# One core, a linear attention and a gated feed-forward layer in float32: blocks 3 to 8 worked in pairs of 1024 tokens, both weights in the seven-product form

## The chip, the core and the metric

The kernel runs on one core of a Trainium2 chip. A core has five engines, each with its own queue of instructions that it works through in order: TensorE (PE, matrix products, with a separate row PEld for loading the stationary operand), VectorE (DVE), ScalarE (ACT), GpSimd (POOL) and SyncE (SP), which here only starts DMA transfers. Engines wait for one another through semaphores. SBUF is the on-chip memory, PSUM the eight banks into which TensorE accumulates, DRAM the memory off the core. The metric is the device time of one execution in microseconds (us); lower is better.

## The reference

```python
kv = np.einsum('bhsd,bhse->bhde', k, v)              # (8, 8, 64, 64)
out = np.einsum('bhsd,bhde->bhse', q, kv)            # no softmax
rms = np.sqrt(np.mean(out * out, axis=-1, keepdims=True) + 1e-06)
x = heads_side_by_side(out / rms * g_norm)           # (8, 576, 512)

h = x.transpose(0, 2, 1) @ U @ V                     # mixing along the 576 tokens, rank 32
u = x + h.transpose(0, 2, 1)
y = u + np.maximum(u @ w_ch1, 0.0) @ w_ch2           # 512 -> 2048 -> 512
```

All is float32. There are 8 batches of 576 tokens, 8 heads of 64 columns; the last line is by far the largest part. The fp32 products are made of three fp32r products each: every operand is split into a high and a low half, and hi*hi + hi*lo + lo*hi is kept.

## The kernel before

**Preparation.** A batch is prepared in four pieces, one per pair of heads (`pair_steps`): `kv` (k^T v, L277), `out` (q times that, L300, then the squares, the sums and the scaling, L303 to L331), `turn` (x is transposed in 32x32 pieces on DVE, L356, and 16 DMAs set the pieces into `ut32`, L359), `xsplit`, `t` (x^T U, L370) and `mix` (times V, L440, and a DVE addition to the turned x, L443). The steps' places are numbers in tables (`STEPS`, `PARTS`, `FIRST_KV`, `OTHER_KV`): so many half-iterations or stages after the start of a block.

**Feed-forward.** The 8*576 = 4608 tokens are worked in 9 blocks of 512, counted from 0 here as `j`. The hidden width of 2048 is cut into 16 chunks `f` of 128. For blocks 0 and 1, a chunk takes 12 matmuls of 512 columns (`ffn1`, L454 to L456: four row groups, three products each), a relu on ACT with the low half on DVE (L463, L464), and 12 matmuls for w_ch2 (`ffn2`, L471). For blocks 2 to 8 the first weight is used in a **seven-product form** (`fast_group`): two chunks and two halves of 256 tokens make a 2x2 problem of blocks, and seven products `P1` to `P7` replace eight. Each product is six matmuls of 256 columns (L607); DVE and ACT put the sums together (L662, L666, L669, L670). Their weight combinations are made in block 1 (`weight_combos`: POOL adds the two halves of each weight, L561; DVE makes four sums, L568), written to DRAM (`wd`) and read again for each block (`wt`, L597). Their token combinations are made by `factor` on DVE and ACT (L543 to L548). The second weight is used plainly there: 12 matmuls of 512 columns per chunk (L625), taken from `queue` between the products; the last block splits the last row group into two halves of 256 columns.

**What sets the order.** From block 2 on TensorE's order is the order of the code. On the other engines, and on TensorE in blocks 0 and 1, a scheduler chooses it when the program is built. SP starts all DMAs in one order; a DMA that waits holds up those behind it.

Of the kernel before, what the change touches and what calls it, by code (L numbers as in the profile page):

```python
# [73 lines left out]
def build(ctx: ExitStack, tc: tile.TileContext, kv_in, kvt0_in, kvt_in, q_in, uv_in, g_in, w_in, out):  # L74
# [20 lines left out]
    uf = const.tile([P, NT, 2 * R], F32, name="uf")  # L95
# [160 lines left out]
    def bank():  # L256
# [3 lines left out]
        return ps_p.tile([P, 512], F32, name="pp")  # L260

# [84 lines left out]

    def turn_step(b, p):
# [6 lines left out]
        else:  # L354
            xt = sc.tile([P, 4, NT, 32], F32, name="xt")
            nc.vector.transpose(out=xt.rearrange("p k i j -> p i k j"), in_=x.rearrange("p i (k j) -> p i k j", j=32))  # L356
            for a in range(4):
                for k in range(4):
                    nc.sync.dma_start(out=ut32[p][32 * k:32 * k + 32, QO[a]:QO[a] + QL[a]],  # L359
                                      in_=xt[32 * a:32 * a + 32, k, 0:QL[a] // 32].rearrange("p i j -> p (i j)"))  # L360

    def t_step(b, p):
        tp = bank()
# [71 lines left out]
    def mix_part(b, p, part):  # L435

        m = S // 2 if b < FAST else BLK * (b + 1) - S * b
        lo, hi = ((0, m), (m, S))[part]
        mp = bank()[:, 0:hi - lo]
        nc.tensor.matmul(mp, lhsT=state[b, p]["t4"], rhs=v4[:, lo:hi], start=True, stop=True)  # L440
        own = ut32[p][:, lo:hi]
        to = x32(b)[:, p, BLK - m:] if b >= FAST and part == 0 else own
        nc.vector.tensor_tensor(out=to, in0=mp, in1=own, op=ALU.add)  # L443
# [34 lines left out]
    def finish_part(part, j):  # L478
        c, cols, acc = part
        o = st.tile([P, DM], F32, name="st")[:, 0:cols.stop - cols.start]  # L480
        if j < FAST:
            uh, ul = ut[j]
            nc.vector.tensor_tensor(out=o, in0=acc, in1=uh[c].bitcast(F32), op=ALU.add)
            nc.gpsimd.tensor_tensor(out=o, in0=o, in1=ul[c].bitcast(F32), op=ALU.add)
# [32 lines left out]
    def ring(i):  # L517
# [8 lines left out]
        if i < 6:  # L526
            return slot(f"w1_{i - 4}", 1)[0]
# [539 lines left out]
```

## Time and profile before

| | |
|---|---|
| median of 3 runs (lowest to highest) | 909.07 us (908.11 to 911.46) |
| the profiled execution: its time / its span | 908.89 us / 907.1 us |
| DMA moved, mean rate | 186.81 MB, 206 GB/s |
| granted TensorE clock | 1.000 |

The span runs from the first to the last instruction of the profiled execution; the time has 1.8 us more around it. The profile's page gives the busy time of every engine, the costliest groups of instructions (line, engine, operation, output and input by the program's names, shape, count, busy time, mean of one, and the idle time before them with what ended it), the chain of work that ended last, and the DMAs. Matmuls overlap in their records, so the cost of one in a row of many is the distance from start to start, not its duration.

### The profile page before, as it was taken

Reading aid. Unit: us, or ns where it says so; the run is one execution under the profiler, and the core shown is the slowest. Engines: PE = TensorE matmul, PEld = TensorE weight load, DVE = VectorE, ACT = ScalarE, POOL = GpSimd, SP = SyncE. Lnnn points to the kernel's source line nnn. Section 1 sums busy time; section 2 is a strip of 40 time slices with the busy share of each in tenths; the row PEclk is TensorE's granted clock in tenths of the full one; section 3 lists DMA queues with packets and bytes.
Section 4 is the critical chain, followed back from the end, with each engine's and each line's share of the span. In section 5 each row is a group of like instructions: output and inputs, shape, how many; then the busy total and the mean of one; then the engine's idle time right before and its main releaser. Section 6 shows DMA issues by size and latency. Waiting matters only on the chain.

```text
span 907.1 us, 15333 instructions
## 1 busy us (share of the span) xinstructions
PE 888.4 (98%) x5540; PEld 788.2 (87%) x5540; DVE 569.8 (63%) x1278; ACT 368.3 (41%) x818; POOL 38.0 (4%) x53
## 2 busy tenths in 40 slices
PE   8899999999999999999999999999999999999997
PEld 7678888887889998899999999999999999998997
DVE  5799987668475577566856586558755662253233
ACT  5677743333244353444533354335332432232221
POOL 2000023212010000000000000000000000000000
PEclk9999999999999999999999999999999999999999
DMA  9966355544756565666665557557744665546541
GB/s 345 417 263 195 101 182 158 182 147 155 268 184 243 223 245 166 229 239 216 221 220 224 183 189 257 179 213 259 262 168 174 215 221 186 163 163 213 180 142 47
DMA packets 76541, 186.81 MB, mean 206 GB/s; under 512 B 12721, under 2 KB 45233, under 8 KB 69297
## 3 DMA queue, kind: packets, MB, share of 16 engines
q1 hardware_dynamic: 76464, 185.82, 58.3%
q8 instruction: 44, 0.72, 0.3%
q14 instruction: 33, 0.26, 0.1%
HBM read 149.73 MB, written 24.12 MB: 192 GB/s over the span
## 4 chain that ended last, share of the span: by engine, by line
PE 82%; DMA 7%; DVE 4%; SPq 3%; ACT 2%; issue 1%; POOL 0%; DVEq 0%; ACTq 0%
PE y L625 31%; PE h L607 15%; PE pp L607 14%; PE y L471 6%; SPq L359 3%; PE h L454 2%; PE pp L277 2%; PE h L455 2%; PE pp L300 2%; PE h L456 2%; DMA out<-st 1%; DMA wt<-wd 1%; DMA wd<-dec 1%; DMA ut<-xt 1%; DMA kvq<-kv_in 1%
## 5 line engine op out<-in xcount | busy, mean ns | idle before, releaser
L607 PE MATMUL h<-uc,wt 128*128 128x256 f32 x1176 | 175.2, 285 | 0.3 <-DVE sums L666 0.3
L625 PE MATMUL y<-hh,ws 128*128 128x512 f32 (+1 forms) x528 | 175.1, 389 | 0.0
L607 PE MATMUL pp<-uc,wt 128*128 128x256 f32 x1176 | 173.1, 283 | 0.1
L607 PEld LDWEIGHTS h<-uc,wt 128*128 128x128 f32 x1176 | 161.2, 190 | 10.2 <-DVE sums L666 0.7
L607 PEld LDWEIGHTS pp<-uc,wt 128*128 128x128 f32 x1176 | 154.9, 191 | 0.5 <-DVE sums L666 0.3
L625 PEld LDWEIGHTS y<-hh,ws 128*128 128x128 f32 x528 | 97.5, 189 | 16.2
L625 PE MATMUL y<-dec,ws 128*128 128x512 f32 (+1 forms) x396 | 103.0, 389 | 0.0
L625 PE MATMUL y<-hl,ws 128*128 128x512 f32 (+1 forms) x264 | 102.8, 389 | 0.0
L666 DVE TENSOR_TENSOR sums<-h,dec 128x256 f32<-128x256 f32 x112 | 47.1, 421 | 64.1 <-PE h L607 63.3
L625 PEld LDWEIGHTS y<-dec,ws 128*128 128x128 f32 x396 | 70.3, 189 | 11.9
L669 ACT ACTIVATE hh<-sums 128x512 fp32r<-128x512 f32 x75 | 47.0, 629 | 80.3 <-DVE sums L666 78.7
L666 DVE TENSOR_TENSOR sums<-pp,dec 128x256 f32<-128x256 f32 x112 | 47.1, 421 | 46.0 <-PE pp L607 39.8
L471 PE MATMUL y<-hh,ws 128*128 128x512 f32 x216 | 71.6, 397 | 0.2 <-ACT hh L463 0.2
L662 ACT COPY dec<-h 128x256 f32<-128x256 f32 x84 | 31.2, 372 | 86.2 <-PE h L607 85.9
L670 DVE SCALAR_TENSOR_TENSOR hl<-sums,hh 128x512 fp32r<-128x512 f32 x75 | 51.9, 692 | 18.9 <-ACT hh L669 18.2
L625 PEld LDWEIGHTS y<-hl,ws 128*128 128x128 f32 x264 | 49.9, 189 | 7.6
L454 PE MATMUL h<-ut,ws 128*128 128x512 f32 x112 | 44.9, 401 | 3.3 <-DVE hl L464 3.3
L471 PEld LDWEIGHTS y<-hh,ws 128*128 128x128 f32 x216 | 39.0, 188 | 8.0 <-issue 0.5
L455 PE MATMUL h<-ut,ws 128*128 128x512 f32 x112 | 43.8, 391 | 0.0
L456 PE MATMUL h<-ut,ws 128*128 128x512 f32 x112 | 43.7, 391 | 0.0
L471 PE MATMUL y<-hl,ws 128*128 128x512 f32 x108 | 42.0, 389 | 0.0
L316 DVE TENSOR_REDUCE sums<-x 128x10 f32<-128x640 f32 x28 | 22.9, 817 | 26.9 <-ACT x L304 26.6
(216 smaller groups left out, 1338.0 us busy)
## 6 DMA issues: line engine op xcount, KB each, us to landing
wt<-wd SPq DMA_DIRECT2D x56, 1024.0 KB, 5.8
wt<-wd SPq DMA_DIRECT2D x56, 768.0 KB, 5.2
kv_sb<-kv_in SPq DMA_DIRECT2D x29, 512.0 KB, 5.1
raw<-w_in SPq DMA_DIRECT2D x14, 1023.6 KB, 15.0
out<-st SPq DMA_DIRECT2D x35, 256.0 KB, 5.1
q_sb<-q_in SPq DMA_DIRECT2D x29, 288.0 KB, 5.6
wd<-ws SPq DMA_DIRECT2D x42, 128.0 KB, 3.8
ut<-xt SPq DMA_DIRECT2D x224, 20.0 KB, 2.1
```

Of the source, the lines that this page charges most:

```text
L316: nc.vector.tensor_reduce(out=sums.rearrange("p (i h) -> p i h", h=2), in_=xv, axis=AX.X, op=ALU.add)
L359: nc.sync.dma_start(out=ut32[p][32 * k:32 * k + 32, QO[a]:QO[a] + QL[a]], in_=xt[32 * a:32 * a + 32, k, 0:QL[a] // 32].rearrange("p i j -> ...
L454: nc.tensor.matmul(h, lhsT=w1s[f][0][:, d, :], rhs=uh[d], start=(d == 0), stop=False)
L455: nc.tensor.matmul(h, lhsT=w1s[f][0][:, d, :], rhs=ul[d], start=False, stop=False)
L456: nc.tensor.matmul(h, lhsT=w1s[f][1][:, d, :], rhs=uh[d], start=False, stop=(d == ND - 1))
L471: nc.tensor.matmul(acc, lhsT=w2s[f][w][:, c, :], rhs=h[:, cols], start=(f == 0 and w == 0 and h is hh), stop=(f == NF - 1 and w == 1))
L607: nc.tensor.matmul(acc, lhsT=w[:, ws_, e * P:(e + 1) * P], rhs=u[:, us, e, :], start=fresh and e == 0 and n == 0, stop=e == 1 and n == 2, ...
L625: nc.tensor.matmul(acc, lhsT=w2s[f][w][:, c, :], rhs=h[:, cols], start=start, stop=stop)
L662: return lambda acc: nc.scalar.copy(out=to, in_=acc)
L666: nc.vector.tensor_tensor(out=to, in0=acc, in1=other, op=ALU.add)
L669: nc.scalar.activation(out=hh, in_=sums[:, 1 - i], func=AF.Relu)
L670: nc.vector.scalar_tensor_tensor(out=hl, in0=sums[:, 1 - i], scalar=0.0, in1=hh.bitcast(F32), op0=ALU.max, op1=ALU.subtract)
```

## The change

- **Three plain blocks instead of two.** Block 2 is now worked like block 1 (`NC = 3`).
- **Blocks 3 to 8 in three pairs.** Within a pair the two halves are blocks of 512 tokens, and both weights are in the seven-product form. `UNITS` lists a pair's work: twice (s = 0 and 1) 28 units of the first weight (`first_unit`, L629) for four groups of two chunks, and then 28 units of the second weight (`second_unit`, L678). A unit is six matmuls of 512 columns.
- **Between the two**, the four hidden blocks of a group are kept as float32 (`hk`), relu is made in place by ACT (L639), POOL makes their combinations (L641, L642, L662, L664), and `make_part`, three units ahead, splits each factor of the second weight into high (ACT) and low (DVE, L660). POOL also adds the products that were set aside (`plus`, L689) and makes the differences of `factor` (L545). The outputs build up in the place of the input (`x32`) and leave from there (L699).
- **Weights.** `weight_combos` now runs for both weights, 16 times instead of 8, from block 1 into block 2; its four sums are POOL's (L579). All seven factors of both weights come from DRAM, four units (1 MB) a transfer, with three buffers (`load_units`, L598).
- **The turned x** goes to DRAM in four DMAs (L373) and comes back in one (L375).
- **Preparation** has new tables: batch 3 and 4 in blocks 1 and 2 (`EARLY`, `STARTS2`), batches 5 and 6 during pair 0, batch 7 during pair 1 (`STARTS`, in units).

```diff
-STEPS = dict(kv=1, out=2, t=8, mix=8, gap=6)
+STEPS = dict(kv=1, out=2, t=5, mix=7, gap=5)
...
+NC = 3
+PAIRS = 3
+KEEP = 4
+FIRST_COMBO = 1
+STARTS = {5: (2, 9, 16, 23), 6: (32, 44, 56, 64), 7: (8, 18, 56, 66)}
+PARTS = dict(kv=0, out=4, turn=8, xsplit=8, t=13, mix0=17, mix1=18)
+EARLY = {(3, 0): (dict(kv=21, out=22, xsplit=22, turn=22), dict(t=0, mix=4)),
+         (3, 1): (dict(kv=26, out=28), dict(xsplit=1, turn=1, t=6, mix=10))}
+STARTS2 = {(3, 2): 1, (3, 3): 9, (4, 0): 17, (4, 1): 25, (4, 2): 33, (4, 3): 41}
...
+USE2 = "P2 P1 P6 P5 P7 P3 P4".split()
+UNITS = [u for s in range(NG // KEEP)
+         for u in [("1", name, KEEP * s + g + i) for g in range(0, KEEP, 2)
+                   for two in (("P1", "P6") if g == 0 else ("P6", "P1"), ("P5", "P7"), ("P3", "P4"), ("P2",))
+                    for i in range(2) for name in two]
+         + [("2", name, KEEP * s + g) for name in USE2 for g in range(KEEP)]]
...
             for a in range(4):
-                for k in range(4):
-                    nc.sync.dma_start(out=ut32[p][32 * k:32 * k + 32, QO[a]:QO[a] + QL[a]],
-                                      in_=xt[32 * a:32 * a + 32, k, 0:QL[a] // 32].rearrange("p i j -> p (i j)"))
+                nc.sync.dma_start(out=xd[:, QO[a]:QO[a] + QL[a]].rearrange("(k j) n -> j k n", k=4),
+                                  in_=xt[32 * a:32 * a + 32, :, 0:QL[a] // 32].rearrange("p k i j -> p k (i j)"))
+            nc.sync.dma_start(out=ut32[p], in_=xd)
...
+        def less(name, a, b):
+            t[name] = st.tile([P, BLK], F32, name="st")
+            nc.gpsimd.tensor_tensor(out=t[name], in0=a, in1=b, op=ALU.subtract)
+            return t[name]
...
-            nc.vector.tensor_tensor(out=o, in0=a, in1=b, op=op)
+            nc.gpsimd.tensor_tensor(out=o, in0=a, in1=b, op=op)
...
+    def first_unit(q, g, name, w):
...
+        for e in range(2):
+            u = place(2 * USE.index(name) + e)
+            for n, (ws_, us) in enumerate(((0, 0), (0, 1), (1, 0))):
+                nc.tensor.matmul(acc, lhsT=w[:, ws_, e * P:(e + 1) * P], rhs=u[:, us], start=fresh and e == 0 and n == 0,
+                                 stop=e == 1 and n == 2, skip_group_check=not fresh)
...
+        if name in copies:
+            nc.scalar.copy(out=copies[name], in_=acc)
+            return
...
+        nc.vector.tensor_tensor(out=to, in0=acc, in1=other, op=ALU.add)
+        nc.scalar.activation(out=to, in_=to, func=AF.Relu)
+        if name == "P2":
+            nc.gpsimd.tensor_tensor(out=h12, in0=h22, in1=h12, op=ALU.subtract)
+            nc.gpsimd.tensor_tensor(out=kept_t(g), in0=h12, in1=h11, op=ALU.add)
...
+    def make_part(q, n):
...
+        nc.scalar.copy(out=hh, in_=src)
+        nc.vector.tensor_tensor(out=hl, in0=src, in1=hh.bitcast(F32), op=ALU.subtract)
+        if name == "P2":
+            nc.gpsimd.tensor_tensor(out=h21, in0=h21, in1=kept_t(g), op=ALU.subtract)
+        elif name == "P1":
+            nc.gpsimd.tensor_tensor(out=h11, in0=h22, in1=kept_t(g), op=ALU.subtract)
...
+    def second_unit(q, n, w):
...
+        def plus(to, s):
+            nc.gpsimd.tensor_tensor(out=to, in0=to, in1=s, op=ALU.add)
...
-    for what in queue:
-        what()
+    for q in range(PAIRS):
+        for n, (which, name, g) in enumerate(UNITS):
+            k = (q * NU + n) // 4
+            if n % 4 == 0:
+                for ahead in range(3):
+                    load_units(k + ahead)
```

How the rows of a queue stand before and after, at three places. First TensorE in the middle of a block. Before, in block 2: products of the first weight (L607, 256 columns) alternate with matmuls of the second (L625, 512 columns).

```order
L607 MATMUL h<-uc,wt 128x256 x6
L607 MATMUL pp<-uc,wt 128x256 x6
L625 MATMUL y<-dec,w2s_451 128x512 x7
L607 MATMUL h<-uc,wt 128x256 x6
L607 MATMUL pp<-uc,wt 128x256 x6
```

After, in pair 0, where the first weight's units (L629) end and the second's (L678) begin, with one piece of preparation (L286, L289, L455, L312) between them:

```order
L629 MATMUL y<-uc,wt 128x512 x6
L286 MATMUL pp<-tails 128x256
L289 MATMUL pp<-kv_sb 128x128 x4
L629 MATMUL y<-uc,wt 128x512 x18
L455 MATMUL h<-v_92,t_4094 128x288
L629 MATMUL y<-uc,wt 128x512 x6
L455 MATMUL h<-v_92,t_4094 128x288
L312 MATMUL pp<-kvb_94,q_sb 128x128 x4
L314 MATMUL pp<-kvb_94,q_sb 128x128
L678 MATMUL y<-hh,wt 128x512
L678 MATMUL y<-hl,wt 128x512
L678 MATMUL y<-hh,wt 128x512 x2
```

All matmuls of the feed-forward now have 512 columns, and the weights of both kinds are the streamed `wt`.

Second POOL. Before, its queue ends in block 2 with the last additions of `weight_combos` and of block 1's output:

```order
L561 TENSOR_TENSOR dec<-ws_1143 128x512
L561 TENSOR_TENSOR dec<-ws_1183 128x512
L561 TENSOR_TENSOR dec<-ws_1232 128x512
L561 TENSOR_TENSOR dec<-ws_1280 128x512
L484 TENSOR_TENSOR st<-st,ut 128x512 x4
```

After, it goes on through all pairs; here in pair 0, from the last group of the first half into its second units (`hk` the kept hidden blocks, `t` their combination, `sp` the products set aside, `x_2631` and `x_2632` the outputs of pair 0, `x_3738` and `x_3739` the input of pair 1):

```order
L642 TENSOR_TENSOR t_3902<-hk 128x512
L662 TENSOR_TENSOR hk<-hk,t_3902 128x512
L664 TENSOR_TENSOR hk<-hk,t_3902 128x512 x4
L689 TENSOR_TENSOR x_2631<-x_2631,sp 128x512 x2
L689 TENSOR_TENSOR x_2632<-x_2632,sp 128x512 x2
L545 TENSOR_TENSOR st<-x_3738 128x512
L689 TENSOR_TENSOR x_2631<-x_2631,sp 128x512 x2
L689 TENSOR_TENSOR x_2632<-x_2632,sp 128x512 x2
L641 TENSOR_TENSOR hk<-hk 128x512 x2
```

POOL has work beside every unit, and one subtraction for pair 1 (L545) stands before the second half's own.

Third SP. Before, the 16 DMAs of a turned x (L359) stand together between two weight transfers (L597):

```order
L597 DMA wt<-wd_98 128x2048
L359 DMA ut_86<-xt 32x160 x8
L359 DMA ut_86<-xt 32x128 x8
L597 DMA wt<-wd_98 128x1536
L183 DMA kv_sb<-kv_in 128x1024
```

After, in pair 0, four DMAs to DRAM (L373), then the one back (L375), which waits for those four; a weight transfer (L598), which waits for TensorE to free its buffer, can stand between them:

```order
L598 DMA wt<-wd_114 128x2048
L373 DMA xd_98<-xt 32x4x160 x2
L373 DMA xd_98<-xt 32x4x128 x2
L598 DMA wt<-wd_115 128x2048
L375 DMA ut_86<-xd_98 128x576
L192 DMA kv_sb<-kv_in 128x1024
```

The trip of a piece has become two transfers, one behind the other, and 5 DMAs stand where 16 stood.

More of the change, by code (lines that the diff above doesn't have):

```diff
@@ L345, in xsplit_step @@
         s["hl"] = (xh, xl)
+    xds = [tc.dram_tile([P, S], F32, name=f"xd{i}") for i in range(2)]
     def turn_step(b, p):
@@ L579, in make_room @@
-    def make_room(i):
-        if i > 0:
-            to = [whole(2 * i, 0, s) for s in range(2)]
+            nc.gpsimd.tensor_tensor(out=o, in0=a, in1=b, op=op)
+        for half, names in enumerate((("P5", "P6"), ("P7", "P3"))):
+            both = (const.tile([P, 2, 2, HALF], F32R, name="sh", tag="top") if half == 0
+                    else dec.tile([P, 2, 2, HALF], F32R, name="dec"))
+            src = t[:, 2 * half:2 * half + 2]
+            nc.scalar.copy(out=both[:, :, 0], in_=src)
+            nc.vector.tensor_tensor(out=both[:, :, 1], in0=src, in1=both[:, :, 0].bitcast(F32), op=ALU.subtract)
+            for k, name in enumerate(names):
+                put(name, None, both[:, k])
@@ L617, in y_of @@
-    def y_of(j):
-        return once(("y", j), lambda: outputs(j))
-    def ffn2_parts(j, hs, first, last):
-        def part(i, f, w, h, start, stop):
-            def run():
-                c, cols, acc = y_of(j)[i]
-                nc.tensor.matmul(acc, lhsT=w2s[f][w][:, c, :], rhs=h[:, cols], start=start, stop=stop)
-                if stop:
-                    finish_part((c, cols, acc), j)
-            return run
-        n = ND + (j == NBLK - 1)
-        halves = [range(2), range(2, n)] if last and len(hs) > 1 else [range(n)]
-        return [part(i, f, w, h, first and f == hs[0][0] and m == 0, last and f == hs[-1][0] and m == 2)
-                for some in halves for f, hh, hl in hs for i in some for m, (w, h) in enumerate(((0, hh), (0, hl), (1, hh)))]
@@ new lines, in at_block @@
+    def at_block(n, what):
+        later.setdefault((None, n), []).append(what)
+    at_block(3, lambda: [nc.gpsimd.tensor_copy(out=x32(0)[p][:, 0:UPPER[2]], in_=side(p)) for p in range(NPAIR)])
+    for (b, p), (_, at) in EARLY.items():
+        for name in at:
+            if name != "mix":
+                at_block(at[name], pair_steps(b, p)[name])
+        at_block(at["mix"], lambda b=b, p=p: mix_step(b, p))
+    for (b, p), start in STARTS2.items():
+        for at, what in pair_steps(b, p).items():
+            at_block(start + PARTS[at], what)
@@ new lines, in build @@
+    at_block(30, lambda: [factor(0, "P1 P2", e) for e in range(2)])
+    at_block(STARTS2[4, 2] + PARTS["mix1"] + 1, lambda: factor(0, "P5 P6 P7 P3 P4", 0))
+    at_block(STARTS2[4, 3] + PARTS["mix1"] + 1, lambda: factor(0, "P5 P6 P7 P3 P4", 1))
+    for b, starts in STARTS.items():
+        for p, start in enumerate(starts):
+            for at, what in pair_steps(b, p).items():
+                at_stage((b - 5) // 2, start + PARTS[at], what)
+    for b, at in CARRY.items():
+        for p in range(NPAIR):
+            at_stage((b - 4) // 2, at, lambda b=b, p=p: carry(b, p))
@@ L947, in build @@
+    for q in range(PAIRS - 1):
+        made = [(names, e) for names in ("P1", "P5 P6 P4", "P7", "P3", "P2") for e in range(2)]
+        for i, (names, e) in enumerate(made):
+            at_stage(q, MAKE[0] + MAKE[1] * i, lambda q=q, names=names, e=e: factor(q + 1, names, e))
     last = {}
```

383 lines of the change are left out of this document (191 added, 192 removed).

## The prediction

> **What bounds the kernel now.** I read the page's busy times and its chain first, then the table of stretches.
>
> ```profile
> PE 888.4 (98%) x5540; PEld 788.2 (87%) x5540; DVE 569.8 (63%) x1278; ACT 368.3 (41%) x818; POOL 38.0 (4%) x53
> PE 82%; DMA 7%; DVE 4%; SPq 3%; ACT 2%; issue 1%; POOL 0%; DVEq 0%; ACTq 0%
> ...
> 100.00:190.00 90.00, 88.88 (x451) 73.19 (x449) 69.70 (x140) 39.17 (x73) 18.05 (x14) 1.00 0.50 159
> 190.00:275.00 85.00, 82.94 (x458) 70.77 (x457) 55.64 (x111) 30.50 (x70) 13.30 (x10) 1.00 0.59 200
> 541.00:630.00 89.00, 89.00 (x599) 81.15 (x599) 56.90 (x136) 36.78 (x89) 0.00 (x0) 1.00 0.63 226
> 718.00:807.00 89.00, 89.00 (x559) 80.44 (x559) 41.35 (x90) 27.48 (x62) 0.00 (x0) 1.00 0.57 185
> ```
>
> A row of the table is a stretch and its length, then the busy time of PE, PEld, DVE, ACT and POOL, the granted clock, the DMA share and GB/s. In the middle of the kernel (541 to 630 us) TensorE is busy all the time at full clock, DVE 64% of it, and POOL does nothing. So time goes where matmuls go, and the other engines count only where they make TensorE wait. The two stretches to 275 us, blocks 1 and 2 of the old kernel, hold the only POOL work of the feed-forward, and TensorE idles there a little.
>
> **What a matmul costs.** The timeline of TensorE and the chain give the distances from start to start.
>
> ```profile
> 226.47 2.73 PE y L471 x12
> 237.36 2.72 PE y L471 x12
> ```
>
> ```profile
> 560.18 0.88 PE L607 MATMUL h<-uc,wt 128*128 128x256 f32 x6
> 560.89 0.88 PE L607 MATMUL pp<-uc,wt 128*128 128x256 f32 x6
> 561.61 1.55 PE L625 MATMUL y<-dec,ws 128*128 128x512 f32 x6
> 563.00 0.28 PE L274 MATMUL pp<-tails 128*128 128x256 f32 x1
> 563.11 1.05 PE L277 MATMUL pp<-kv_sb 128*128 128x128 f32 x8
> 563.92 0.31 PE L440 MATMUL pp<-v,t 128*128 128x128 f32 x1
> ```
>
> Twelve matmuls of 512 columns take 2.72 us of the chain: **0.227 us** each. Six of 256 columns take 561.61 - 560.89 = 0.72 us, or 0.715 by the mean of both rows: **0.119 us** each, over half of the other. (With their neighbours in between, six of 512 took 1.39 us, 0.232 each; the new units change bank as often, so I leave this out on both sides.)
>
> **The change, part 1: TensorE's work.** By the code, blocks 2 to 8 now hold 7 x 336 = 2352 matmuls of 256 columns (8 groups, 7 products, 6 each) and 7 x 192 = 1344 of 512 columns, 48 of them cut in two. That is 2352 x 0.119 = 279.9 us, and 1344 x 0.2268 + 48 x 0.011 = 305.3 us: 585.2 us. The new kernel has a third plain block, 384 x 0.2268 = 87.1 us, and three pairs with 112 units of 6, 2016 x 0.2268 = 457.2 us: 544.3 us. The difference is **-40.9 us**. Preparation keeps its matmuls. The gain has two sources: the second weight saves an eighth in six blocks, and 256 columns are no longer paid at over half of 512; block 2 gives some of it back. Since TensorE has no idle time to lose in the middle, all of it comes off the end, unless a new wait takes its place.
>
> **Part 2: POOL, and what it does to DVE.** This is where the profile speaks against the change. POOL's groups and one place in block 1:
>
> ```profile
> L561 POOL TENSOR_TENSOR dec<-ws 128x512 f32<-128x512 f32 x14 | 18.5, 1339 | 70.8 <-DVE dec L572 70.8
> L484 POOL TENSOR_TENSOR st<-st,ut 128x512 f32<-128x512 f32 x8 | 10.3, 1306 | 34.5 <-DVE st L483 34.5
> L543 DVE TENSOR_TENSOR t<-x,t 128x256 f32<-128x256 f32 x36 | 15.0, 417 | 0.6
> L321 DVE TENSOR_TENSOR ta<-ta,r 128x10 f32<-128x10 f32 x28 | 4.7, 168 | 0.6
> ```
>
> ```profile
> 207.88 2.84 POOL L561 TENSOR_TENSOR dec<-ws 128x512 f32<-128x512 f32 x2 [14.21 <-DVE dec L572]
> ...
> 208.18 1.40 DVE L543 TENSOR_TENSOR t<-x 128x256 f32<-128x256 f32 x1
> ...
> 209.50 1.24 DVE L320 TENSOR_TENSOR ta<-r,half 128x10 f32<-128x10 f32 x1
> ...
> 210.86 0.68 DVE L464 SCALAR_TENSOR_TENSOR hl<-h,hh 128x512 fp32r<-128x512 f32 x1
> ...
> 211.60 0.50 PE L454 MATMUL h<-ut,ws 128*128 128x512 f32 x1 [1.40 <-DVE hl L464]
> ```
>
> While POOL adds (207.88 to 210.72), a DVE subtraction that is worth 0.417 us takes 1.40, and one of ten columns, worth 0.168, takes 1.24. Both read two operands from SBUF. The next, L464, reads one from PSUM and takes its ordinary 0.68, but it stood behind them, and TensorE waited 1.40 us for it. So each POOL operation can cost DVE about 1 us if DVE meets it with such an instruction. The Trainium skill, page "SBUF — State Buffer", section "Who interferes with whom", has it as a lock: DVE with two SBUF inputs and a GpSimd instruction that reads SBUF take turns, and the second fully blocks. The rows agree.
>
> The new kernel counts 204 POOL operations of 128x512 (32 in `weight_combos`, 24 in `factor`, 96 on the kept blocks, 48 in `plus`, 4 at block 0's output) where 24 stood, and 64 of 128x256. The wide ones cost 1.31 to 1.34 us. No row has the narrow ones: they cost something between nothing and the 1.34 us of the wide ones, and I take half of these, 0.7, since they do half of the same work. That is 268 + 45 = 313 us where 32 were.
>
> *Blocks 1 and 2.* Sixteen combinations take 16 x (2 x 1.34 + 4 x 0.7) = 88 us of POOL where 8 x 2.68 = 21 stood, and four outputs move to DVE. What POOL cost TensorE so far:
>
> ```profile
> PEld h L454 <- DVE hl L464: 5.9, 7, 1.8
> ```
>
> 5.9 us in seven waits is an upper bound, as some have other causes; nothing is the lower. PE's own row of L454 puts 3.3 us to it.
>
> ```profile
> L454 PE MATMUL h<-ut,ws 128*128 128x512 f32 x112 | 44.9, 401 | 3.3 <-DVE hl L464 3.3
> ```
>
> With 67 us more POOL work beside two blocks, by ratio, 3.3 x 67 / 32 = 7 and 5.9 x 67 / 32 = 12; I take **+8 us**, from 3 to 20.
>
> *Pairs.* A unit takes 6 x 0.227 = 1.36 us. Per second unit DVE makes one low half, from two SBUF operands; per first unit at most one addition out of PSUM, which POOL doesn't hold up. The nearest rows:
>
> ```profile
> L170 DVE TENSOR_TENSOR xl<-x,xh 128x512 fp32r<-128x512 f32 x24 | 16.3, 678 | 2.8 <-ACT xh L158 2.8
> L329 DVE TENSOR_TENSOR x<-pp,half 128x512 f32<-128x512 f32 x28 | 19.3, 689 | 1.1
> L670 DVE SCALAR_TENSOR_TENSOR hl<-sums,hh 128x512 fp32r<-128x512 f32 x75 | 51.9, 692 | 18.9 <-ACT hh L669 18.2
> L669 ACT ACTIVATE hh<-sums 128x512 fp32r<-128x512 f32 x75 | 47.0, 629 | 80.3 <-DVE sums L666 78.7
> ```
>
> ACT has one operation of 0.63 us per unit and is no bound. The fullest stage for DVE is pair 0, with eight pieces of preparation. A piece costs DVE, by the last two stretches above, (56.90 - 41.35) / (136 - 90) x 16 instructions = 5.4 us, and TensorE some 2.8 (0.9 for kv by the rows from 563.00 on, as much for out, half a microsecond for t, the rest mix). Pair 0 takes TensorE 112 x 1.36 + 8 x 2.8 = 175 us. DVE has 56 x 0.68 + 32 x 0.69 + 14 x 0.69 + 16 x 0.7 = 81 us, and 8 x 5.4 = 43: 124. POOL's 56 operations, met at a random point, add half of 1.31 each, 37 us: 161 of 175. It fits, with little to spare. Parts are made three units (4.1 us) ahead, so single waits are covered; a crowded stretch is not. Pairs 1 and 2, with four pieces and none, stay at 81 + 22 + 37 = 140 of 164 and at 71 + 31 = 102 of 152. I take **+6 us** for all three, from 0 to the rival's 52 below.
>
> **Part 3: the streams.** A transfer of four units brings 1 MB in 4 x 1.36 = 5.4 us, with two buffers ahead.
>
> ```profile
> wt<-wd SPq DMA_DIRECT2D x56, 1024.0 KB, 5.8
> ...
> q_sb<-q_in SPq DMA_DIRECT2D x29, 288.0 KB, 5.6
> ...
> ut<-xt SPq DMA_DIRECT2D x224, 20.0 KB, 2.1
> ```
>
> Before, 1.75 MB came per group of 42 x 0.119 + 24 x 0.227 = 10.4 us, 168 KB per us; now 188. A transfer lands 5.8 us after its issue and has 10.8 us. The x that goes through DRAM needs two landings, 2.1 and about 5.6 (the one back is as large as a q), 7.7 us, plus at most one weight transfer between them on SP, 5.4: 13.1. From turn to mix there are 9 units, 12.3 us, and some preparation in between, 1 to 3 us. It just fits, so nothing is charged.
>
> **Part 4: ends.** Into pair 0 the first unit has TensorE's spare bank, and ACT's first copy waits for block 2's last chunk (2.7 us) with two units between; at the end the last output leaves in pieces of 256 instead of 128 KB. I take **+2 us** together, from 0 to 6.
>
> **The sum.** 907.1 - 40.9 + 8 + 6 + 2 = 882.3 us of span, and 1.8 us around it (908.89 - 907.1): **884 us**. The profiled run lies 0.2 us under the median of 909.07, so nothing is corrected.
>
> **Rivals.**
> *Slower: POOL and DVE take turns in earnest.* In the second 28 units of the second half of pairs 0 and 1, DVE has 28 x 0.68 + 14 x 0.69 = 28.7 us with two SBUF operands and POOL 24 x 1.31 = 31.4 us (8 on the hidden blocks, 8 `plus`, 8 in `factor`): in turns 60 us, beside 38.1 us of TensorE. That is 22 us over, twice; the other second halves have 16 POOL operations and are over by 2 each, 8 in all: +52 in the place of my +6, **930 us**. It decides once the excess of a stretch passes the 4.1 us of lead and the work can't move into the first units, where DVE reads PSUM. For it: the 1.40 and 1.24 us above. Against it: POOL's order has some of `factor` standing earlier, and POOL's late results are needed only units later. It is what the lock in the Trainium skill's page "SBUF — State Buffer" comes to here, taken at its word.
> *The gain mostly eaten by the x trip.* DVE waits in order for the x that comes back.
>
> ```profile
> DVE ut L443 <- DMA ut<-xt: 12.8, 8, 2.7
> ...
> DVE x L443 <- DMA ut<-xt: 4.6, 4, 2.1
> ```
>
> Now that is 17.4 us in 12 waits, hidden behind DVE's slack. If 13 us and more become usual, the 20 pieces from batch 3 on wait 1 to 2 us each, with DVE near full in pair 0: +20, **904 us**.
> *Nothing waits.* If the lead covers all of POOL, only the ends stay, 884 - 8 - 6: **870 us**.
>
> **Chances and range.** Forecast (871 to 898) 0.62; nothing waits (below 871) 0.08; the trip (898 to 912) 0.16; taking turns (912 to 940) 0.14. The range of 868 to 910 leaves out about 0.18: the last, the top of the trip, and little below. A measurement of this kernel can tell 0.5% from no change, 904.5 to 913.6 us. Faster: 0.62 + 0.08 + half of the trip, 0.78; within it: the other half, 0.08; slower: taking turns, 0.14.
>
> **What will show it.** Right: 512-column matmuls at 0.227 us through the pairs, a pair of about 153 us without and 175 us with preparation, DVE at 75 to 90% in pair 0, POOL near 310 us busy. In blocks 1 and 2, waits of TensorE for L482 of about 8 us. Wrong: waits of L678 for L660 with POOL busy beside them (the slower rival), DVE waiting at L462 for the transfer back (the trip), or L629 and L678 waiting for `wt`, which I left out.

## The result and the profile after

The changed kernel takes **923.69 us** (median of 4 runs, 923.10 to 924.11) against 908.86 us before in the same session: a ratio of 1.0158 with a 95% interval of 1.0137 to 1.0179. It is 14.8 us slower; 884 us were forecast. The time lies beside the 930 us of the rival "POOL and DVE take turns in earnest", which had a chance of 0.14.

First the page of the changed kernel, its busy times and its chain, as the prediction showed them of before.

```profile
PE 864.7 (94%) x4196; PEld 704.4 (76%) x4196; DVE 671.2 (73%) x1099; ACT 463.1 (50%) x890; POOL 357.8 (39%) x301
PE 47%; DVE 17%; DMA 2%; issue 2%; ACT 1%; SPq 0%; POOL 0%; DVEq 0%; ACTq 0%
```

The span is 921.1 us, against 907.1. TensorE's work did become less, but it is now busy 94% instead of 98% of the span, and DVE's share of the chain went from 4% to 17%. DVE executes fewer instructions than before (1099 for 1278), yet is busy 101 us longer: its instructions got longer, not more. The groups show which; of each the busy time, then the mean in ns.

```profile
L660 DVE TENSOR_TENSOR hl<-hk,hh 128x512 fp32r<-128x512 f32 x72 | 72.9, 1027 | 12.9 <-ACT hh L659 12.0
L660 DVE TENSOR_TENSOR dec<-hk,dec 128x512 fp32r<-128x512 f32 x72 | 67.6, 946 | 9.0 <-ACT dec L659 8.9
L660 DVE TENSOR_TENSOR dec<-t,dec 128x512 fp32r<-128x512 f32 x12 | 19.1, 1618 | 2.8 <-ACT dec L659 2.8
L554 DVE SCALAR_TENSOR_TENSOR uc<-st,g_sb,uc 128x512 fp32r<-128x512 f32 x24 | 30.3, 1264 | 1.9 <-ACT uc L553 1.8
L638 DVE TENSOR_TENSOR hk<-y,sp 128x512 f32<-128x512 f32 x92 | 62.7, 688 | 68.6 <-PE y L629 56.2
L689 POOL TENSOR_TENSOR x<-x,sp 128x512 f32<-128x512 f32 x48 | 75.6, 1598 | 68.3 <-DVE x L695 55.2 <-ACT sp L704 11.1 <-DVE half L334 2.0
```

L638 has one operand in PSUM and takes the 0.69 us that I had for all of them. L660 and L554 read two operands from SBUF and take 0.95 to 1.62 us. POOL's own additions went up as well, L689 from the 1.31 of the prediction to 1.60.

Next the view of TensorE's waits (total, times, longest).

```profile
PE y L678 <- DVE hl L660: 15.2, 8, 3.8
PE h L475 <- DVE hl L482: 9.5, 6, 4.0
PE h L455 <- DVE x L462: 8.6, 6, 4.2
```

All three are waits for DVE. The first is the sign that the prediction named for the slower rival; the second, 9.5 us, is near the 8 us that it named for its own forecast. The timeline in pair 0 shows how the first comes about (start, duration, instruction):

```profile
531.66 1.76 DVE L554 SCALAR_TENSOR_TENSOR uc<-st,g_sb,uc 128x512 fp32r<-128x512 f32 x1
533.35 0.74 DVE L554 SCALAR_TENSOR_TENSOR uc<-x,g_sb,uc 128x512 fp32r<-128x512 f32 x1
534.01 1.74 DVE L660 TENSOR_TENSOR hl<-hk,hh 128x512 fp32r<-128x512 f32 x1
535.68 1.77 DVE L554 SCALAR_TENSOR_TENSOR uc<-st,g_sb,uc 128x512 fp32r<-128x512 f32 x1
537.37 1.75 DVE L660 TENSOR_TENSOR hl<-hk,hh 128x512 fp32r<-128x512 f32 x1
```

```profile
533.57 1.64 POOL L545 TENSOR_TENSOR st<-x,x 128x512 f32<-128x512 f32 x1 [0.69 <-DVE uc L554]
535.17 1.73 POOL L642 TENSOR_TENSOR t<-hk 128x512 f32<-128x512 f32 x1
536.86 1.72 POOL L662 TENSOR_TENSOR hk<-hk,t 128x512 f32<-128x512 f32 x1
```

```profile
535.81 0.50 PE L678 MATMUL y<-hl,wt 128*128 128x512 f32 x1 [3.81 <-DVE hl L660]
```

From 534 us on each DVE instruction ends about half a microsecond after the POOL one that started before it, and the next of each starts at once: one pair per 1.7 us, where DVE alone needs 0.69. A second unit of TensorE needs one L660 per 1.36 us; with one L554 in between, DVE delivers one in 3.4 us. Ahead of the L660 that ends at 535.75 two L554 stood, and TensorE stood still for 3.81 us.

In blocks 1 and 2 the same happens on a smaller scale:

```profile
197.10 1.17 DVE L332 TENSOR_TENSOR ta<-r,half 128x10 f32<-128x10 f32 x1
198.30 1.20 DVE L333 TENSOR_TENSOR ta<-ta,r 128x10 f32<-128x10 f32 x1
...
200.62 0.67 DVE L482 SCALAR_TENSOR_TENSOR hl<-h,hh 128x512 fp32r<-128x512 f32 x1
```

```profile
196.95 2.53 POOL L571 TENSOR_TENSOR dec<-ws 128x512 f32<-128x512 f32 x2 [1.46 <-DVE dec L585]
```

```profile
201.35 0.50 PE L475 MATMUL h<-ut,ws 128*128 128x512 f32 x1 [2.38 <-DVE hl L482]
```

Two DVE instructions of ten columns, worth 0.17 us each, take 1.17 and 1.20: they end when the two POOL additions end, at about 198.2 and 199.5. L482 stands behind them and three more of the same piece of preparation, and TensorE waits 2.38 us.

The balance over the whole span: I summed, over all neighbouring matmuls, the distance from start to start less the bare one (0.227 us for 512 columns, 0.119 for 256). Gaps over 0.3 us went from 16.2 to 59.5 us, time at half clock from 0 to 7.0, smaller delays from 20.3 to 25.7: 92.2 us above the bare matmuls instead of 36.5, so 55.7 more. The span grew by 14.0, so the bare matmuls saved 41.7, at the prediction's own prices for one matmul. The prediction had 40.9.

### The profile page after: what moved, and what is told of

The parts are those of the page before. It is cut to its first block, busy times and chain, and to the rows that moved or that the text cites. A ratio compares the mean times of both kernels' runs of the same rounds, so it can differ in the third digit from the quotient of the medians.

```text
span 921.1 us, 12302 instructions
## 1 busy us (share of the span) xinstructions
PE 864.7 (94%) x4196; PEld 704.4 (76%) x4196; DVE 671.2 (73%) x1099; ACT 463.1 (50%) x890; POOL 357.8 (39%) x301
## 4 chain that ended last, share of the span: by engine, by line
PE 47%; DVE 17%; DMA 2%; issue 2%; ACT 1%; SPq 0%; POOL 0%; DVEq 0%; ACTq 0%
PE y L629 18%; PE y L678 15%; PE y L489 4%; DVE dec L660 4%; DVE hl L660 4%; DVE uc L554 2%; PE pp L312 2%; DVE hk L638 1%; PE pp L289 1%; PE h L475 1%; PE h L476 1%; PE h L477 1%; DMA out<-x 1%; DVE x L693 1%; DVE xt L370 1%
## 5 line engine op out<-in xcount | busy, mean ns | idle before, releaser
L629 PE MATMUL y<-uc,wt 128*128 128x512 f32 x966 | 229.9, 393 | 1.0 <-ACT sp L635 1.0
L629 PEld LDWEIGHTS y<-uc,wt 128*128 128x128 f32 x966 | 178.7, 188 | 37.9 <-ACT sp L635 1.4
L678 PE MATMUL y<-dec,wt 128*128 128x512 f32 x504 | 128.8, 399 | 1.4 <-DVE dec L660 0.7
L678 PEld LDWEIGHTS y<-dec,wt 128*128 128x128 f32 x504 | 94.2, 191 | 27.9 <-DVE dec L660 9.0
L678 PE MATMUL y<-hh,wt 128*128 128x512 f32 x336 | 114.0, 397 | 0.0
L638 DVE TENSOR_TENSOR hk<-y,sp 128x512 f32<-128x512 f32 x92 | 62.7, 688 | 68.6 <-PE y L629 56.2
L641 POOL TENSOR_TENSOR hk<-hk 128x512 f32<-128x512 f32 x24 | 31.6, 1316 | 184.4 <-ACT hk L639 184.4
L689 POOL TENSOR_TENSOR x<-x,sp 128x512 f32<-128x512 f32 x48 | 75.6, 1598 | 68.3 <-DVE x L695 55.2
L639 ACT ACTIVATE hk<-hk 128x512 f32<-128x512 f32 x96 | 60.3, 630 | 52.9 <-DVE hk L638 51.6
L678 PE MATMUL y<-hl,wt 128*128 128x512 f32 x168 | 68.2, 406 | 15.6 <-DVE hl L660 15.2
L660 DVE TENSOR_TENSOR hl<-hk,hh 128x512 fp32r<-128x512 f32 x72 | 72.9, 1027 | 12.9 <-ACT hh L659 12.0
L660 DVE TENSOR_TENSOR dec<-hk,dec 128x512 fp32r<-128x512 f32 x72 | 67.6, 946 | 9.0 <-ACT dec L659 8.9
L678 PEld LDWEIGHTS y<-hh,wt 128*128 128x128 f32 x336 | 64.2, 191 | 12.8
L489 PEld LDWEIGHTS y<-hh,ws 128*128 128x128 f32 x336 | 62.0, 188 | 15.3 <-ACT hh L481 3.1
L475 PE MATMUL h<-ut,ws 128*128 128x512 f32 x168 | 67.0, 399 | 5.1 <-DVE hl L482 5.1
L579 POOL TENSOR_TENSOR dec<-dec 128x256 f32<-128x256 f32 x64 | 48.9, 784 | 33.2 <-DMA wd<-dec 26.1
```

The costliest lines, as they stand in the source:

```text
L475: nc.tensor.matmul(h, lhsT=w1s[f][0][:, d, :], rhs=uh[d], start=(d == 0), stop=False)
L489: nc.tensor.matmul(acc, lhsT=w2s[f][w][:, c, :], rhs=h[:, cols], start=(f == 0 and w == 0 and h is hh), stop=(f == NF - 1 and w == 1))
L579: nc.gpsimd.tensor_tensor(out=o, in0=a, in1=b, op=op)
L629: nc.tensor.matmul(acc, lhsT=w[:, ws_, e * P:(e + 1) * P], rhs=u[:, us], start=fresh and e == 0 and n == 0, stop=e == 1 and n == 2, skip_g ...
L638: nc.vector.tensor_tensor(out=to, in0=acc, in1=other, op=ALU.add)
L639: nc.scalar.activation(out=to, in_=to, func=AF.Relu)
```

## The experiments

Fourteen kernels, each timed in three rounds against the kernel before. Times are medians in us; the changed kernel has 923.7.

| run | us | ratio to before (95%) |
|---|---|---|
| one_operand | 896.9 | 0.9861 (0.9842 to 0.9879) |
| no_read | 905.1 | 0.9953 (0.9935 to 0.9971) |
| both_out | 878.6 | 0.9659 (0.9637 to 0.9681) |
| plus_psum | 916.2 | 1.0082 (1.0051 to 1.0113) |
| pairs_dve | 912.7 | 1.0046 (1.0026 to 1.0066) |
| combos_dve | 922.3 | 1.0146 (1.0121 to 1.0170) |
| combos_all_dve | 923.2 | 1.0152 (1.0136 to 1.0168) |
| r_st | 920.8 | 1.0125 (1.0108 to 1.0143) |
| x_direct | 951.4 | 1.0460 (1.0440 to 1.0479) |
| small | 916.9 | 1.0086 (1.0063 to 1.0109) |
| halves_plus | 904.7 | 0.9951 (0.9929 to 0.9973) |
| small_plus | 892.8 | 0.9827 (0.9798 to 0.9855) |
| small_plus_r_st | 895.2 | 0.9843 (0.9821 to 0.9864) |
| small_best | 901.2 | 0.9913 (0.9891 to 0.9934) |

one_operand, no_read and both_out leave out part of the arithmetic; the others make all outputs.

### Is it the second operand?

```diff
-        nc.vector.tensor_tensor(out=hl, in0=src, in1=hh.bitcast(F32), op=ALU.subtract)
+        with nc.allow_low_precision(reason="copy"):
+            nc.vector.tensor_reduce(out=hl, in_=hh.bitcast(F32).rearrange("p (i j) -> p i j", j=1), axis=AX.X, op=ALU.add)
```

> The subtraction of L660, which makes the low half of a second unit's x, is replaced by a reduction over a length of 1 that reads hh alone (so the low half is hh itself; the outputs differ from the reference). The 168 instructions keep about their length, 0.65 us in the nearest row (L328, 640 elements in 0.82), but have one operand in SBUF. Theory, DVE and POOL take turns where DVE reads two SBUF operands: L660 comes to 0.6 to 0.7 us each, TensorE's waits for L660 (15.2 us by the view of waits, with what they cost in half clock) nearly go, POOL's L545 and L642 fall from 1.6 and 1.3 us towards 1.2, and the time comes to 885 to 905 us. Rival, DVE is simply too full in these stretches, or POOL's results come late: L660 may get shorter, but the waits move to another line and the time stays at 915 to 924 us.

896.9 us, 26.8 less than the changed kernel. The groups of this run, where the line is L661:

```profile
L661 DVE TENSOR_REDUCE dec<-dec 128x512 fp32r<-128x512 f32 x84 | 57.1, 681 | 28.2 <-ACT dec L659 28.0
L661 DVE TENSOR_REDUCE hl<-hh 128x512 fp32r<-128x512 f32 x84 | 57.0, 683 | 25.8 <-ACT hh L659 25.2
```

All 168 take 0.68 us, with POOL's work unchanged beside them. The stretch in which both engines have most to do, the last 28 units of pair 1, as a row of the table of stretches (PE, PEld, DVE, ACT, POOL busy, clock), of the changed kernel and of one_operand:

```profile
708.90:761.10 52.20, 42.10 (x172) 30.69 (x171) 46.05 (x44) 24.02 (x41) 33.10 (x21) 1.00 0.50 156
```

```profile
700.00:739.00 39.00, 38.78 (x172) 31.57 (x171) 28.25 (x43) 23.20 (x41) 28.95 (x21) 1.00 0.65 212
```

52.2 us against 39.0, with practically the same instructions. DVE falls from 46.1 to 28.3 us, POOL from 33.1 to 29.0: the 22 us that both lose are time spent waiting for each other inside instructions, which the profile counts as busy. That DVE was simply too full with work of its own is excluded for this stretch. The instruction with one SBUF operand is free beside POOL, as the Trainium skill has it (page "SBUF — State Buffer", section "Who interferes with whom": with at most one SBUF input, and outside the modes of DVE that use two ports, there is no contention); the 0.68 us agree.

### Blocks 1 and 2: POOL's reads, or the buffers and DMAs?

```diff
-            nc.gpsimd.tensor_tensor(out=r[:, k], in0=whole(2 * i + k, n, 0).bitcast(F32), in1=whole(2 * i + k, n, 1).bitcast(F32),
-                                    op=ALU.add)
+            nc.gpsimd.memset(r[:, k], 0.001)
...
-            nc.gpsimd.tensor_tensor(out=o, in0=a, in1=b, op=op)
+            nc.gpsimd.memset(o, 0.001)
```

> In the weight combinations (blocks 1 and 2) POOL's 32 additions at L571 and 64 sums at L579 become memsets of the same tiles: POOL reads no SBUF there, while the buffers, the order and the DMAs stay (the combined weights are left out, so the outputs differ from the reference). The pairs are as in the changed kernel. Theory, a DVE operation with two SBUF operands waits for a whole POOL operation also here (a 10-element one of L332 takes up to 1.18 us instead of 0.17): L332 and L333 come back to about 0.17 us, TensorE's waits of L475 for L482 (9.5 us) fall below 4, and 10 to 16 us go: 907 to 914 us. Rival, the two dec buffers and the DMAs that read them make the waits of blocks 1 and 2: the time stays at 917 to 924 us, with L475's waits as they were.

905.1 us, 18.6 less, a little under the range of the theory. The view of the tile `ta` in blocks 1 and 2 (minimum, median and maximum in ns), of the changed kernel and of no_read, and no_read's waits of L475:

```profile
L332 DVE TENSOR_TENSOR ta<-r,half x12: 170/384/1178, 120.4 to 336.0; 128x10 f32<-128x10 f32 x12
```

```profile
L332 DVE TENSOR_TENSOR ta<-r,half x13: 170/170/172, 119.7 to 333.7; 128x10 f32<-128x10 f32 x13
```

```profile
PE h L475 <- DVE hl L482: 2.8, 4, 0.9
```

POOL still writes the same tiles, but DVE no longer waits for it. That POOL's reads count and its writes do not is what the Trainium skill says too (page "SBUF — State Buffer", section "Who interferes with whom"), and the 0.17 us of no_read agree. A memset is shorter than an addition, so part of the 18.6 us may come from the shorter chain of a combination. The buffers were tried by themselves:

```diff
-        r = dec.tile([P, 2, DM], F32, name="dec")
+        r = [st.tile([P, DM], F32, name="st") for _ in range(2)]
```

> The sums r of the weight combinations are held in two buffers of the pool st instead of one of dec, so that dec is left to t and the second pair of results, and POOL need not wait for the DMAs that read it. Theory of turns: L579's waits for DMA (26.1 us) fall, yet L332 still takes up to 1.2 us and the time stays within 918 to 924 us. Rival, the wait for the DMAs, which ACT and DVE inherit, is what costs blocks 1 and 2: 908 to 916 us.

920.8 us. POOL's waits for DMA at L579 are gone (19.1 us of other waits stay), and L333 still takes up to 1.25 us: the buffers are worth about 3 us. How the rest divides between the reads and the shorter chain, neither run separates; small_best, below, bears on it. Moving POOL's work to DVE was no way out:

```diff
-            nc.gpsimd.tensor_tensor(out=o, in0=a, in1=b, op=op)
+            nc.vector.tensor_tensor(out=o, in0=a, in1=b, op=op)
```

> The four sums of a weight combination at L579 go back from POOL to DVE, where the kernel before had four of this length. Theory, in blocks 1 and 2 ACT and DVE stand behind POOL's sums, which wait for the DMAs that still read dec: ACT's wait of L584 for L579 (19.0 us) falls below 8, the half-clock stretches at 202, 260 and 274 us go, and the time comes to 912 to 918 us; the pairs stay as they are. Rival: DVE gets 28 us more and waits itself for dec's DMAs, with relu's low half (L482) behind that wait: 922 to 935 us.

> Both the additions of L571 and the sums of L579 are on DVE, about 32 x 0.68 + 64 x 0.42 = 49 us more for it in blocks 1 and 2; POOL has only four copies there. The sums alone moved the time by 1.4 us, since L571, whose operations are the longer, stayed. Theory: the long operations of L571 were what DVE met; L332 comes to 0.17 us and 6 to 12 us go: 911 to 918 us. Rival, DVE is full in blocks 1 and 2 (it had 66 to 75% of them): 922 to 935 us.

922.3 and 923.2 us (combos_all_dve changes the additions of L571 in the same way). Both lie at the lower edge of the rival's range, and both theories were half right. In combos_dve ACT's wait did not go, it changed its cause: 24.8 us for DVE's L579, which now waits for `dec`'s DMAs itself. In combos_all_dve L332 took 0.17 us at most, so the turns were gone, and the wait of L475 fell from 9.5 to 5.0 us; others took its place:

```profile
PE pp L312 <- DVE x L462: 3.7, 1, 3.7
PE pp L312 <- DVE x L341: 3.1, 1, 3.1
...
115.00:225.00 110.00, 105.34 (x513) 84.71 (x513) 91.64 (x198) 42.11 (x89) 6.74 (x4) 1.00 0.58 190
```

DVE is busy 91.6 of 110 us there, instead of 74.7.

### Do both together explain the miss?

> one_operand and no_read in one kernel: the second units' low half reads one SBUF operand, and POOL reads no SBUF in blocks 1 and 2 (what both leave out is left out here). Theory, the missed time of the prediction is what DVE and POOL cost each other: the gains of 26.8 and 18.6 us add up, 923.7 - 45.4 = 878, 874 to 884 us, and the rest of the prediction's sum (870 where nothing waits) holds. Rival, another cost, now hidden behind these waits, comes up: 886 to 896 us.

878.6 us: the two gains, 26.8 and 18.6, add up to 45.4, and 45.1 came. The page:

```profile
PE 848.1 (97%) x4196; PEld 703.1 (80%) x4196; DVE 580.1 (66%) x1099; ACT 461.9 (53%) x890; POOL 271.6 (31%) x301
```

So what the two edits take out is the bulk of the miss: without its terms of +6 and +8 the prediction had 870 us, and 878.6 were measured. The 8.6 us left lie mainly in pair 0. The three pairs in the same columns as above, of the changed kernel and of both_out:

```profile
374.10:576.70 202.60, 189.43 (x925) 153.56 (x924) 164.61 (x270) 110.50 (x224) 82.84 (x56) 0.97 0.62 210
576.70:761.10 184.40, 169.82 (x794) 136.55 (x794) 136.22 (x189) 95.86 (x179) 85.30 (x56) 1.00 0.59 199
761.10:916.80 155.70, 155.28 (x672) 124.99 (x671) 92.60 (x105) 75.40 (x124) 72.04 (x48) 1.00 0.56 194
```

```profile
358.60:554.20 195.60, 186.03 (x926) 153.54 (x926) 146.38 (x270) 110.06 (x224) 75.75 (x56) 0.98 0.65 218
554.20:721.20 167.00, 165.85 (x794) 137.61 (x793) 109.68 (x189) 95.08 (x179) 75.57 (x56) 1.00 0.65 221
721.20:873.20 152.00, 152.00 (x672) 125.96 (x671) 69.85 (x105) 75.39 (x124) 61.13 (x48) 1.00 0.57 198
```

In both_out pairs 1 and 2 take 167 and 152 us, the 164 and 152 of the prediction's working; pair 0 takes 195.6 instead of 175. These 20.6 us are more than the 8.6, because the 870 carried along some 10 us of delays of the kernel before (worked out under "Why the prediction was wrong"), of which pairs 1 and 2 keep little. The last 28 units of pair 0 hold no matmul of preparation and still take 45.3 us (508.9 to 554.2), where pair 2 takes 38. L660 no longer takes turns there, but L554, which kept its two operands, does:

```profile
513.41 1.78 DVE L554 SCALAR_TENSOR_TENSOR uc<-st,g_sb,uc 128x512 fp32r<-128x512 f32 x1
515.12 1.74 DVE L554 SCALAR_TENSOR_TENSOR uc<-x,g_sb,uc 128x512 fp32r<-128x512 f32 x1
...
517.51 0.50 PE L678 MATMUL y<-hl,wt 128*128 128x512 f32 x1 [2.81 <-DVE hl L660]
```

### The trip through DRAM

```diff
-                nc.sync.dma_start(out=xd[:, QO[a]:QO[a] + QL[a]].rearrange("(k j) n -> j k n", k=4),
-                                  in_=xt[32 * a:32 * a + 32, :, 0:QL[a] // 32].rearrange("p k i j -> p k (i j)"))
-            nc.sync.dma_start(out=ut32[p], in_=xd)
+                for k in range(4):
+                    nc.sync.dma_start(out=ut32[p][32 * k:32 * k + 32, QO[a]:QO[a] + QL[a]],
+                                      in_=xt[32 * a:32 * a + 32, k, 0:QL[a] // 32].rearrange("p i j -> p (i j)"))
```

> The turned x goes straight from SBUF to SBUF again in 16 transfers for each group of heads, as in the kernel before, instead of through DRAM. Theory that the trip costs the gain: 905 to 916 us. Theory that POOL and DVE cost it: DVE waits 3.1 us in all for what comes back, so the time stays at 921 to 926 us, with TensorE's waits for L660 as they were.

951.4 us, which neither theory had. The trip doesn't cost the gain, it saves 28 us. SP's timeline for one piece, of x_direct and of the changed kernel:

```profile
98.16 10.01 SPq L373 DMA_DIRECT2D ut<-xt  x16
```

```profile
89.75 1.88 SPq L373 DMA_DIRECT2D xd<-xt  x4
...
99.73 0.45 SPq L375 DMA_DIRECT2D ut<-xd  x1
```

Sixteen issues hold SP's queue for 10.0 us here, five for 2.3. SP now also issues the stores of the combined weights and a megabyte of `wt` every 5.4 us, and these stand behind. In x_direct TensorE waits 7.6 us for `wt`, and POOL's L578 waits 56.6 us for the DMAs that read `dec` (26.1 in the changed kernel). That the issues are the cause is read from these waits; how the 28 us divide among them was not tried. I had priced the landings of the trip (13.1 us), but not the issues that it takes off the queue.

### Fewer and shorter turns

```diff
-            nc.gpsimd.tensor_tensor(out=to, in0=to, in1=s, op=ALU.add)
...
+            nc.vector.tensor_tensor(out=to, in0=a, in1=to, op=ALU.add)
...
-                nc.scalar.copy(out=copies[name][:, c], in_=acc[c])
```

> The 48 additions of L689 on POOL, 75.6 us busy at 1.6 us each, and the copies that ACT makes for them (L704) go; DVE adds the banks P1, P6 and P5 straight from PSUM to each place where they are needed, the same sums in another order, 24 more DVE instructions of about 0.69 us each. Theory of turns: POOL's work in the second halves of the pairs falls by more than a third, L660 gets shorter, TensorE waits less: 903 to 914 us. Rival, DVE is bound by its own work: some 35 us more of DVE, in bursts at the ends of the second halves, where the banks are also held longer: 925 to 935 us.

916.2 us, 7.5 less; the theory's range missed by 2. Here `a` is the bank in PSUM, so the 24 additions more take 0.68 us each, free beside POOL. L660's first group falls to 0.84 us on average; the twelve of `hl<-t,hh` still take 1.47, beside POOL's remaining work.

> As plus_psum, and the combinations of the pairs (L545, L641, L642, L662, L664: 120 operations) move from POOL to DVE, at about 0.69 us each, 83 us more for DVE; POOL has nothing in the pairs. All outputs are made as before. Theory of turns: L660 and L554 come to 0.69 us, DVE's own excess in the second halves of pairs 0 and 1 (about 49 us of work beside 38 of TensorE) is partly taken up elsewhere: 893 to 905 us, and POOL's share, not DVE's work, was the cost. Rival, DVE bound by its own work: 915 to 930 us.

912.7 us, between the two ranges. L660 comes to 0.69 us and L554 to 0.75, so the turns are gone from the pairs. But DVE pays with work of its own: TensorE still waits for L660, 8.9 us in all, and blocks 1 and 2 are as they were (L475 9.5 us). Shorter operations on POOL are the other way:

```diff
+        for c in range(0, out.shape[-1], P):
+            nc.gpsimd.tensor_tensor(out=out[:, c:c + P], in0=in0[:, c:c + P], in1=in1[:, c:c + P], op=op)
```

> POOL's additions and subtractions that the change brought or keeps (L545, L571, L579, L641, L642, L662, L664, L689) are cut into pieces of 128 columns, on POOL still, same results. Theory, a DVE operation with two SBUF operands waits for the end of whatever operation POOL has begun: it now waits 0.4 us at most where it waited 1.2, so L332 stays below 0.5 us, L482 and L660 come in time, and some 8 to 18 us go: 905 to 916 us. POOL's own busy time does not fall, as its operations only get shorter. Rival, the time in which both need the second operand's way stays the same, and DVE now loses once for each of four pieces: 920 to 935 us.

916.9 us, 6.8 less and just above the theory's range. L332 (here L337) takes 0.51 us at most, but four pieces cost POOL more than one whole (0.48 us and more each, against 1.31), and in this kernel POOL becomes late itself: DVE's L698, which adds products out of the banks, waits 12.4 us for it. TensorE's longest wait, 6.2 us to 742.38, ends 0.1 us after an L698, as if it had waited for that bank; the profile names no releaser. With `plus` gone POOL has the room:

> plus_psum with POOL's remaining operations in pieces of 128 columns. If the two gains add up, 916.2 less 6 to 15: 901 to 910 us. If DVE loses once for each piece: 914 to 928 us.

**892.8 us**: the best complete version, 1.7% under the kernel before. The two edits bring 7.5 and 6.8 us alone, and 30.9 together. Its tile `ta` and its waits:

```profile
L337 DVE TENSOR_TENSOR ta<-r,half x13: 170/171/489, 120.0 to 336.7; 128x10 f32<-128x10 f32 x13
...
PE h L480 <- DVE hl L487: 5.8, 5, 2.6
PE y L683 <- DVE dec L665: 5.0, 10, 1.3
PE y L683 <- DVE hl L665: 1.8, 4, 0.9
```

> small_plus with pieces of 256 columns instead of 128. Theory, the wait of a DVE operation is the length of POOL's operation: between 916.2 (512) and 892.8 (128), nearer to the latter, 895 to 906 us. Rival, with the plus gone it is the number of pieces that matters, or only pieces below some size help: 911 to 918 us.

904.7 us, between 916.2 and 892.8 as expected. Its row of the ten-column operation:

```profile
L337 DVE TENSOR_TENSOR ta<-r,half x12: 148/170/639, 121.5 to 335.3; 128x10 f32<-128x10 f32 x12
```

The longest time of this operation goes with the length of POOL's: 1.18 us at 512 columns, 0.64 at 256, 0.49 at 128, 0.17 without reads. So DVE waits for the operation under way, not for POOL's whole queue.

> small_plus with r of the weight combinations in the pool st. In small_plus ACT still waits 25 us for POOL's sums (L589), TensorE 5.8 us for L487. If the buffers matter once the turns are short: 886 to 891 us; if not, 891 to 895 us.

> pairs_dve (nothing on POOL in the pairs), r_st's buffers, and the weight combinations of blocks 1 and 2 on POOL in pieces of 128 columns. The pairs as in pairs_dve; in blocks 1 and 2 up to the 18 us that no_read brought. Theory: 899 to 907 us. Rival, pieces bring nothing: 909 to 913 us.

895.2 us for small_plus_r_st: no gain from the buffers any more. And 901.2 us for small_best: 11.5 us less than pairs_dve. Here POOL still reads SBUF in blocks 1 and 2, and its chain is no shorter, only its single operations are. With some 3 us for the buffers, 8 to 9 us are left that shorter turns alone bring there. small_best differs from small_plus_r_st only in who makes the combinations of the pairs, DVE or POOL in pieces: there POOL in small pieces does 6 us better than none at all.

## Why the prediction was wrong

**Part 1, -40.9 us: right.** The bare matmuls saved 41.7 by the tally, and where nothing waits, in pair 2 of both_out, 672 matmuls take 152.0 us, 0.226 each.

**Part 2, pairs, +6 us: this step failed, in size.** In the changed kernel the pairs take 202.6, 184.4 and 155.7 us, from each first matmul of L629 to the next. From this go 3 x 152.4 for the units, 12 pieces of preparation at 2.8 and 2.7 for block 2's last chunk: 49 us are left over. Some 10 of them are not new: in the same tally the kernel before, from 341 us on, where its block 3 begins, lies some 10 us above its bare matmuls (under 2 in gaps, the rest in smaller delays), and the sum carried these along in the 907.1. So the increase is about 39 us, where I had 6.

The failed sentence is "161 of 175. It fits, with little to spare." The single delays were priced about right (L660 and L554 lost 83 us beside POOL's 160 operations in the pairs, 0.52 each; I had half of 1.31), but I added them up over a whole pair of 175 us. POOL does not have work beside every unit, as the text ahead of the prediction has it: by the table of stretches it starts 8 to 14 operations beside the 28 first units of a half and 14 to 21 beside the 28 second ones. So the delays crowd into the second units, most of all of the second half, where DVE and POOL have 60 us of work beside 38 of TensorE. My rival counted by these 28 units and came to +52. Both numbers stood in the text, and I took the one averaged over the stage; the lead of three units, 4.1 us, covers single waits, not 22 us of excess. What speaks for the rival's way of counting is the row above: 52.2 us in the changed kernel, 39.0 once L660 reads one operand (the rival had 60 there; the stretch holds 21 POOL operations instead of its 24). Its price was too high all the same: these 28 units are over the bare 38.1 by 14.1 us in pair 1 and by 12.4 in pair 0, where it had 22 each. In pair 0 one_operand takes only 5.3 of the 12.4 away, since L554 keeps its two operands. With L660 the turns account for 27 of the 49 us.

**Part 2, blocks 1 and 2, +8 us: too small.** Without POOL's reads 18.6 us go. The increase can be read from the tally by place. In the first 115 us both kernels have some 11 us of gaps. From there to block 3 (341 us before, 374.1 after) the gaps went from about 4 to 17.6 us, with about 4 us of half clock on top: some 18 us more, where I had 8. In no_read about 6 are left. TensorE's waits for L482, which I had in mind, are only 8.6 of it. The scaling by POOL's busy time missed that the new sums feed a chain: ACT waited 19.0 us for L579, with relu behind it. What this chain cost TensorE was not tried by itself. The two terms together missed by 33 + 10 us, a little more than the 39.7 that the forecast was off; the remaining few us, with the opposite sign, are within what such a tally can tell.

**The clock was missing.** I costed a wait at its own length. After a gap of some 2.2 us and more TensorE can run at half clock; at 537 to 543 us the table of stretches has:

```profile
540.00:541.00 1.00, 1.00 (x3) 0.77 (x3) 1.00 (x2) 0.00 (x0) 1.00 (x2) 0.50 0.00 0
541.00:543.60 2.60, 2.15 (x6) 1.18 (x5) 2.60 (x3) 0.62 (x1) 2.60 (x2) 0.50 0.00 0
```

This makes 7.0 us over the span.

**Part 3, 0: right in the sum, wrong about its worth.** DVE's waits at L462 for the way back are 3.1 us in all, in three waits, and TensorE never waited for `wt`. (The 168 KB per us of before count a MB as 1000 KB, the 188 after as 1024; alike they are 172 and 188. And the sum of the span is 882.2, not 882.3. Neither changes the forecast.) But the trip is not merely free: without it the kernel would be 28 us slower. The rival "x trip" is refuted.

**Part 4, +2 us:** not separated by any run. It is within the 8.6 us that both_out lies above the 870 of "nothing waits". Most of these are in pair 0. Its last 28 units are 7 us over the 38 of pair 2, and there TensorE's waits stand behind L554, which still takes 1.0 to 1.1 us on average beside POOL; the three quarters before (150.3 us, less 3 x 38.1, eight pieces of preparation at 2.8 and the 2.7 above) are some 11 us over, and what makes these stays open.

## What to carry to other kernels

Work moved to an engine that "has room" is priced in the densest stretch, not over a stage: there, count DVE instructions with two SBUF operands and POOL operations that read SBUF as one queue, and compare its length with what the bound engine does meanwhile. Here this count of 60 us was an upper bound (52.2 measured), but far nearer than the average. Where both must run, let DVE take one operand from PSUM, and cut POOL's operations short, as long as POOL has the time for it. A busy share doesn't tell waiting from working: look first at groups whose mean has grown while their shape has not.

## What the runs showed of the hardware

A gap well under the length of the slow phase can halve the clock. After the wait of 2.38 us that ends at 201.35, matmuls come 0.42 us apart from 202.8 to 205.8, about 3.4 us in all with the passage:

```profile
202.79 0.63 PE L477 MATMUL h<-ut,ws 128*128 128x512 f32 x1
203.22 0.63 PE L475 MATMUL h<-ut,ws 128*128 128x512 f32 x1
...
205.78 0.41 PE L489 MATMUL y<-hl,ws 128*128 128x512 f32 x1
```

The Trainium skill (page "TensorE: Matmul & The Clock Gate", section "HAM oscillation — how this bites in real kernels") puts the limit at gaps of about 3.4 us; here 2.38 were enough, and the measurement decides. Yet the 52.2 us of pair 1 above, with 10.1 us of idle time, kept a clock of 1.00, so it isn't the sum of idle time that counts. Nor is it the length of the gap alone: in the changed kernel a gap of 2.17 us that ends at 273.8 was followed by 3.4 us at half clock, and in pairs_dve one of 2.94 us that ends at 635.5 was not. What else decides, no run shows.

Two edits worth 7 us each were worth 31 together. The 12.4 us of waits for POOL in small suggest why: shorter operations need POOL to have room, and fewer of them leave that room.
